# A fused attention and MLP kernel: five engine queues ordered by a list scheduler, softmax sums taken from a column of V, and merges, broadcasts and transposes moved to DMA

## Chip, cores, metric

One core of a Trainium2 chip. The metric is device time in microseconds (us) of one execution. The kernel before takes 318.04 us (median of 4 runs, 317.15 to 318.21).

Engines are named as in the profile: PE is TensorE (PEld its weight loads), DVE VectorE, ACT ScalarE, POOL GpSimd, SP the engine that issues most DMAs. Each engine has its own queue of instructions, and one that waits at the head of its queue holds up those behind it (below, DVE from 7.4 to 18.87 us in the control). A run counts as slow when it is over 1.5% above the fastest of the same kernel; comparisons use fast runs.

## The reference

x is normalised (layernorm, 2048 x 512) to xn; the output is x plus attention of xn plus an MLP of xn.

```python
# attention: 32 heads of 16, 4 segments of 512 positions, causal inside a segment
for s in range(N):
    logits = einsum('bhqd,bhkd->bhqk', qs, ks) * scale + mask
    a_dot = einsum('bhqk,bhkd->bhqd', softmax(logits), vs)
    pq = phi(qs)                         # phi(t) = t+1 if t>0 else exp(t)
    num = einsum('bhld,bhde->bhle', pq, M)
    den = einsum('bhld,bhd->bhl', pq, z)[..., None] + 1e-06
    outs.append(g * num / den + (1.0 - g) * a_dot)      # g = sigmoid(beta)
    M = M + einsum('bhld,bhle->bhde', phi(ks), vs)
    z = z + einsum('bhld->bhd', phi(ks))
o = concat(outs) @ wo
# MLP: silu(xn @ w1) @ w2, w1 is 512 x 1792
return x + o + mlp
```

## The kernel before

Scores are kept transposed (keys on partitions). Four heads are scored at once into `psS`, which fills four banks of PSUM (TensorE's output memory; the program divides it into eight), and one exp of 128x2048 empties it; there are 80 such quads, five for each of 16 groups (4 segments x 4 head groups). Both kernels have this loop and only one `psS`, so score, exp, next score form a serial chain.

```python
def s_quad(st, dt, quad, tiles):
    psS = psatt.tile([P, 4, L], F32, name="psS")
    ...  # 4 or 8 row-tiled matmuls
    Pt = ppool.tile([P, 4, L], BF16, name="Pt")
    nc.scalar.activation(out=Pt[:], in_=psS[:], func=AF.Exp, scale=SCALE)
    ...  # POOL masks the diagonal blocks a little later
```

The softmax sums are a second pass of one-hot matmuls over the same probabilities; the reciprocals are taken on 128x512 and replicated over the 16 rows of a head by matmuls with `sel`:

```python
def z_part(st, dt, tiles):          # as long as the product with V itself
    for par in (1, 0):
        for kt in KTS:
            for g in range(4):
                nc.tensor.matmul(psZ[32*g:32*g+32, kt*P:L], lhsT=oneh[:, 2*dt+par, :],
                                 rhs=p_view(tiles, par, g, kt), ...)
    ...
    nc.vector.reciprocal(out=rec[:], in_=zf[:])

def norm_fill(s, st):               # for each head group dt
    nc.tensor.matmul(psD, lhsT=sel[:, 1, dt, :], rhs=rec[:])   # 1/den, replicated
    pq = phiQT * psD
    nc.tensor.matmul(psR, lhsT=sel[:, 0, dt, :], rhs=rec[:])   # 1/sum, replicated
    a_t = N_sb * psR
    # later: psN = Mbf.T @ pq on PE, oT = a_t + psN on DVE
```

(`norm_fill` is shortened here.) PE's order is made by a cooperative loop: after each quad, generators are pulled until a virtual clock of PE time has passed 2.43 us; small work of other engines is delayed by `later(ns, fn)`.

The softmax here doesn't subtract the row's maximum and nothing guards it: scores larger than these inputs give would overflow.

Of the kernel before, what the change touches and what calls it, by code (L numbers as in the profile page):

```python
# [10 lines left out]
ALU = mybir.AluOpType  # L11
# [17 lines left out]
EPS = 1e-5  # L29

HRING = 23
FILL_NS = 2000
WARM = 44
# [3 lines left out]
def kernel(  # L37
# [17 lines left out]
    cpool = ctx.enter_context(tc.tile_pool(name="cpool", bufs=1))  # L55
    segp = ctx.enter_context(tc.tile_pool(name="segp", bufs=2))
    ppool = ctx.enter_context(tc.tile_pool(name="ppool", bufs=8))
    hpool = ctx.enter_context(tc.tile_pool(name="hpool", bufs=HRING))
    work = ctx.enter_context(tc.tile_pool(name="work", bufs=2))
    xpool = ctx.enter_context(tc.tile_pool(name="xpool", bufs=3))  # L60
    pp = ctx.enter_context(tc.tile_pool(name="pp", bufs=3, space=bass.MemoryType.PSUM))
    psz = ctx.enter_context(tc.tile_pool(name="psz", bufs=1, space=bass.MemoryType.PSUM))
    psatt = ctx.enter_context(tc.tile_pool(name="psatt", bufs=1, space=bass.MemoryType.PSUM))
    ctx.enter_context(tc.manual_schedule(engines={ENG.PE}))


    xts = {}

    def load_x(s, half):
        xt = xpool.tile([P, 2, D], BF16, name="x_in")  # L70
        r0 = s * L + half * 256
        nc.sync.dma_start(
            out=xt[:], in_=x_flat[r0 : r0 + 256, :].rearrange("(two p) d -> p two d", p=P)
        )
        xts[(s, 2 * half)] = xt[:, 0, :]
        xts[(s, 2 * half + 1)] = xt[:, 1, :]

    wk_sb = cpool.tile([P, DT, D], BF16, name="wk_sb")
    wq_sb = cpool.tile([P, DT, D], BF16, name="wq_sb")
    wv_sb = cpool.tile([P, DT, D], BF16, name="wv_sb")  # L80
    wo_sb = cpool.tile([P, DT, D], BF16, name="wo_sb")
    w1_sb = cpool.tile([P, DT, F], BF16, name="w1_sb")
    w2_sb = cpool.tile([P, FT, D], BF16, name="w2_sb")
    load_x(0, 0)
    load_x(0, 1)
    for dst, src in ((wk_sb, A_wk), (wq_sb, A_wq), (wv_sb, A_wv)):
        nc.sync.dma_start(out=dst[:], in_=src.rearrange("(ko ki) n -> ki ko n", ki=P))
    load_x(1, 0)
    for dst, src in ((w1_sb, B_w1), (wo_sb, A_wo), (w2_sb, B_w2)):
        nc.sync.dma_start(out=dst[:], in_=src.rearrange("(ko ki) n -> ki ko n", ki=P))  # L90
    load_x(1, 1)


    ident = cpool.tile([P, P], BF16, name="ident")
    make_identity(nc, ident[:])
    lnc = cpool.tile([P, 2, 2], F32, name="lnc")
    nc.gpsimd.memset(lnc[:, :, 0:1], EPS)
    nc.gpsimd.memset(lnc[:, :, 1:2], -0.5)

    pm_odd = cpool.tile([P, 1], F32, name="pm_odd")  # L100
    nc.gpsimd.memset(pm_odd[:], 1.0)
    for g in range(4):
        nc.gpsimd.memset(pm_odd[32 * g : 32 * g + 16, :], 0.0)




    clock = {"vt": 0.0, "n": 0}
    held = []

    def run_due():
        while held and held[0][0] <= clock["vt"]:
            heapq.heappop(held)[2]()

    def pe(ns):
        clock["vt"] += ns
        run_due()

    def later(ns, fn):
        clock["n"] += 1  # L120
        heapq.heappush(held, (clock["vt"] + ns, clock["n"], fn))


    xnT = {}
    mv_all = cpool.tile([P, NT, nc.vector.BN_AGGR_DIM], F32, name="mv_all")
    rstd_all = cpool.tile([P, NT, 1], F32, name="rstd_all")

    def ln_stats(s, half):
        t0 = s * TPS + 2 * half
        for j in range(2):  # L130
            stats = work.tile([P, nc.vector.BN_STATS_DIM], F32, name="stats")
            nc.vector.bn_stats(out=stats[:], in_=xts[(s, 2 * half + j)])  # L132
            nc.vector.bn_aggr(out=mv_all[:, t0 + j, :], in_=stats[:])
        rs = rstd_all[:, t0 : t0 + 2, :]
        nc.gpsimd.tensor_tensor(
            out=rs, in0=mv_all[:, t0 : t0 + 2, 1:2], in1=lnc[:, :, 0:1], op=ALU.add
        )
        nc.gpsimd.tensor_tensor(out=rs, in0=rs, in1=lnc[:, :, 1:2], op=ALU.pow)

    def ln_norm(s, j):  # L140
        t = s * TPS + j
        xn_t = work.tile([P, D], BF16, name="xn_t")
        nc.vector.tensor_scalar(  # L143
            out=xn_t[:], in0=xts[(s, j)],
            scalar1=mv_all[:, t, 0:1], scalar2=rstd_all[:, t, 0:1],
            op0=ALU.subtract, op1=ALU.mult,
        )
        return xn_t

    def ln_tr(s, j, xn_t, on_act=False):  # L150
        if s not in xnT:
            xnT[s] = segp.tile([P, DT, L], BF16, name="xnT")
        ptr = pp.tile([P, 4, P], BF16, name="ptr", tag="ps")
        for dt in range(DT):
            nc.tensor.transpose(ptr[:, dt, :], xn_t[:, dt * P : (dt + 1) * P], ident[:])  # L155
        pe(300)
        dst = xnT[s][:, :, j * P : (j + 1) * P]
        if on_act:
            nc.scalar.copy(out=dst, in_=ptr[:, :, :])
        else:  # L160
            nc.vector.tensor_copy(out=dst, in_=ptr[:, :, :])

    ln_done = set()

    def ln_fill(s):
        ln_stats(s, 0)
        ln_stats(s, 1)
        prev = None
        for j in range(TPS + 1):
            yield  # L170
            if prev is not None:
                ln_tr(s, j - 1, prev)
            prev = ln_norm(s, j) if j < TPS else None
        ln_done.add(s)


    def gemm4(lhsTs, rhss):
        ps = pp.tile([P, L], F32, name="ps", tag="ps")
        for ki in range(DT):
            nc.tensor.matmul(  # L180
                ps[:, :], lhsT=lhsTs(ki), rhs=rhss(ki), start=(ki == 0), stop=(ki == DT - 1)
            )
        pe(860)
        return ps

    def phi_part(src, dst, after, acc=None):
        ek = work.tile([P, L], BF16, name="ek")
        nc.scalar.activation(out=ek[:], in_=src, func=AF.Exp)  # L188

        def mn():  # L190
            nc.gpsimd.tensor_scalar(  # L191
                out=ek[:], in0=ek[:], scalar1=1.0, scalar2=0.0, op0=ALU.min, op1=ALU.max
            )
            later(800, fin)

        def fin():
            nc.vector.scalar_tensor_tensor(  # L197
                out=dst, in0=src, scalar=0.0, in1=ek[:], op0=ALU.max, op1=ALU.add, accum_out=acc
            )
            if after is not None:  # L200
                later(1000, after)

        later(900, mn)

    vts = []
    for i in range(2):
        vts.append(cpool.tile([P, TPS, H // 2, 3, DH], BF16, name=f"V{i}"))

    def start_proj(s, st):
        st["kT"] = segp.tile([P, DT, L], BF16, name="kT")  # L210
        st["kTo"] = segp.tile([P, DT, L], BF16, name="kTo")
        st["qT"] = segp.tile([P, DT, L], BF16, name="qT")
        st["V"] = vts[s % 2]
        if s < NSEG - 1:
            st["phiK"] = segp.tile([P, TPS, D], BF16, name="phiK", bufs=1)
            st["zc"] = segp.tile([P, DT], F32, name="zc")
        if s > 0:
            st["phiQT"] = segp.tile([P, DT, L], BF16, name="phiQT")

    def k_tile(s, st, dt):  # L220
        ps = gemm4(lambda ki: wk_sb[:, ki, dt * P : (dt + 1) * P], lambda ki: xnT[s][:, ki, :])
        kT, kTo = st["kT"], st["kTo"]
        if s == 0:
            nc.scalar.copy(out=kT[:, dt, :], in_=ps[:, :])
            nc.vector.tensor_scalar(  # L225
                out=kTo[:, dt, :], in0=ps[:, :], scalar1=pm_odd[:, 0:1], scalar2=None, op0=ALU.mult
            )
        else:
            nc.vector.tensor_copy(out=kT[:, dt, :], in_=ps[:, :])
            later(  # L230
                800,
                lambda: nc.gpsimd.tensor_scalar(
                    out=kTo[:, dt, :], in0=kT[:, dt, :], scalar1=pm_odd[:, 0:1], scalar2=1.0,
                    op0=ALU.mult, op1=ALU.mult,
                ),
            )
        if s < NSEG - 1:
            phiKT = work.tile([P, L], BF16, name="phiKT")

            def k_transposes():  # L240
                ptr = pp.tile([P, 4, P], BF16, name="ptr", tag="ps")
                for j in range(TPS):
                    nc.tensor.transpose(ptr[:, j, :], phiKT[:, j * P : (j + 1) * P], ident[:])
# [25 lines left out]
    def proj_fill(s, st, dt0=0):  # L269
        if dt0 == 0:  # L270
            start_proj(s, st)
# [492 lines left out]
```

## Time and profile before

| | before |
|---|---|
| start of the first exp | 21.8 us |
| start of the last exp | 276.4 us, so 254.6 / 79 = 3.22 us per exp |
| end of the last exp to the end of the span | 37.7 us |
| PE, ACT, DVE, POOL busy | 84, 63, 57, 43% |

First the page: busy time of each engine, the clock granted to PE in 40 slices (in tenths of full speed; 9 is 90% or more), the chain of work that ended last, and the exp group (count, then busy us and mean ns of one, then the idle time before it and what ended it).

```profile
span 316.0 us, 6029 instructions
## 1 busy us (share of the span) xinstructions
PE 265.2 (84%) x2496; PEld 117.2 (37%) x2496; DVE 179.7 (57%) x306; ACT 198.0 (63%) x172; POOL 137.0 (43%) x254
...
PEclk9589999999999799999997999999999999997999
...
PE 56%; DVE 22%; POOL 9%; issue 5%; ACT 5%; DMA 1%; POOLq 0%; ACTq 0%
...
L466 ACT ACTIVATE Pt<-psS 128x2048 bf16<-128x2048 f32 x80 | 150.1, 1876 | 57.4 <-PE psS L458 54.0
```

PE is the busiest and has most of the chain, and ACT waited 54.0 us for scores. Next, the stretch from first to last exp and the tail, from the windows view (columns: length in us, then busy us and instructions of each engine, granted clock, share of the 16 DMA engines, GB/s):

```profile
core 0: us, PE busy (x) PEld busy (x) DVE busy (x) ACT busy (x) POOL busy (x), PEclk, DMA share, GB/s
21.80:276.40 254.60, 223.85 (x2235) 96.54 (x2234) 148.51 (x259) 188.79 (x161) 118.56 (x185) 0.99 0.05 17
278.30:316.00 37.70, 29.98 (x182) 13.01 (x179) 18.31 (x24) 3.67 (x6) 1.09 (x1) 0.95 0.11 35
```

And from the timeline the shortest repeat of the loop (start us, length us, engine, line, operation, and the idle time before it):

```profile
140.71 1.88 ACT L466 ACTIVATE Pt<-psS 128x2048 bf16<-128x2048 f32 x1 [1.15 <-PE psS L458]
...
142.70 0.40 PE L458 MATMUL psS<-qT,kT 16*128 16x512 bf16 x4
...
143.20 1.88 ACT L466 ACTIVATE Pt<-psS 128x2048 bf16<-128x2048 f32 x1 [0.62 <-PE psS L458]
```

Where PE is ready, exps start 2.5 us apart: 1.88 us of exp and a gap of 0.62 us in which the score is made. The average is 3.22 us. The other 0.7 us is put down mostly to PE being occupied with something else when the next score is due; PE's 56% of the chain fits that.

### The profile page before, as it was taken

To read this page: it belongs to the slowest core of one execution; us is meant where nothing else is said; L and a number is where in the kernel's file an instruction comes from. 1 tells how busy PE (TensorE), PEld (TensorE's weight loads), DVE (VectorE), ACT (ScalarE), POOL (GpSimd) and SP (SyncE) were. 2 spreads that over 40 slices of the span, in tenths; PEclk is the share of its full clock that TensorE was granted. 3 is DMA by queue.
4 is the path that set the end of the run, shared out by engine and by line. 5 is a ranking of instruction groups with operands and counts; after the bars stand their busy time and mean duration, and the time that the engine had idled before them with its cause. 6 is when DMAs were issued, how large, how long until landed. Compare 5 with 4: busy or idle time off the path is not lost.

```text
span 316.0 us, 6029 instructions
## 1 busy us (share of the span) xinstructions
PE 265.2 (84%) x2496; PEld 117.2 (37%) x2496; DVE 179.7 (57%) x306; ACT 198.0 (63%) x172; POOL 137.0 (43%) x254
## 2 busy tenths in 40 slices
PE   5277869999977887899987889899989799997993
PEld 4122434443433433344333334344423243442441
DVE  3469998877475659411476474751565523237642
ACT  1048658988977497566993856676766578833000
POOL 4995647967333479533231244843323223310000
PEclk9589999999999799999997999999999999997999
DMA  6990010000000000021100000002020011020003
GB/s 220 385 340 21 0 36 33 2 3 0 2 0 2 0 3 1 2 68 33 35 0 2 0 3 0 2 0 68 2 66 2 0 35 34 2 68 0 0 0 100
DMA packets 11403, 12.44 MB, mean 39 GB/s; under 512 B 881, under 2 KB 10865, under 8 KB 11377
## 3 DMA queue, kind: packets, MB, share of 16 engines
q1 hardware_dynamic: 11376, 12.07, 11.8%
q8 instruction: 19, 0.31, 0.4%
q14 instruction: 8, 0.06, 0.1%
HBM read 9.97 MB, written 2.10 MB: 38 GB/s over the span
## 4 chain that ended last, share of the span: by engine, by line
PE 56%; DVE 22%; POOL 9%; issue 5%; ACT 5%; DMA 1%; POOLq 0%; ACTq 0%
PE ps L180 15%; PE psO L401 12%; PE psS L458 6%; PE psZ L519 5%; PE psO_3943 L401 4%; PE psPV L500 4%; DVE hT L301 4%; PE psO L410 3%; ACT Pt L466 2%; ACT th L295 2%; POOL w_sb L570 2%; DVE rec L541 2%; DVE stats L132 2%; DVE phiKT L197 2%; DVE phiQT L197 2%
## 5 line engine op out<-in xcount | busy, mean ns | idle before, releaser
L466 ACT ACTIVATE Pt<-psS 128x2048 bf16<-128x2048 f32 x80 | 150.1, 1876 | 57.4 <-PE psS L458 54.0
L478 POOL TENSOR_SCALAR_AFFINE_SELECT Pt<-Pt 128x512 bf16<-128x512 bf16 (+1 forms) x112 | 77.9, 708 | 120.9 <-ACT Pt L466 120.8
L180 PE MATMUL ps<-xnT,w_sb 128*128 128x512 bf16 x224 | 57.9, 391 | 8.1 <-DVE hT L301 7.5
L301 DVE SCALAR_TENSOR_TENSOR hT<-th,ps 128x512 bf16<-128x512 bf16 x56 | 37.5, 680 | 34.8 <-ACT th L295 34.3
L401 PE MATMUL psO<-w_sb,hT 128*128 128x512 bf16 x168 | 41.9, 383 | 0.0
L295 ACT ACTIVATE th<-ps 128x512 bf16<-128x512 f32 x56 | 32.9, 598 | 7.8 <-DVE hT L301 4.7
L401 PEld LDWEIGHTS <-hT 128*128 128x128 bf16 x224 | 21.2, 99 | 31.2 <-issue 9.1
L180 PEld LDWEIGHTS <-w_sb 128*128 128x128 bf16 x224 | 19.6, 99 | 34.8 <-issue 18.7
L458 PE MATMUL psS<-qT,kTo 32*128 32x512 bf16 (+3 forms) x256 | 17.7, 308 | 4.3 <-ACT Pt L466 2.6
L416 DVE TENSOR_TENSOR o_t<-psO,x_res 128x512 bf16<-128x512 f32 x12 | 8.2, 685 | 21.9 <-PE psO L410 21.9
L519 PE MATMUL psZ<-Pt,oneh 128*32 128x128 bf16 (+3 forms) x512 | 20.3, 300 | 0.0
L180 PE MATMUL ps<-xnT,wq_sb 128*128 128x512 bf16 x64 | 16.7, 384 | 3.5 <-DVE qT L259 3.5
L180 PE MATMUL ps<-xnT,wk_sb 128*128 128x512 bf16 x64 | 17.3, 395 | 1.9 <-DVE kTo L225 1.2
L458 PE MATMUL psS<-qT,kT 16*128 16x512 bf16 (+3 forms) x256 | 17.1, 300 | 1.1 <-ACT Pt L466 1.1
L191 POOL TENSOR_SCALAR ek<-ek 128x512 bf16<-128x512 bf16 x24 | 15.5, 651 | 4.1 <-ACT ek L188 4.1
L180 PE MATMUL ps<-wv_sb,xnT 128*128 128x512 bf16 x64 | 16.0, 379 | 1.3 <-DVE N_sb L509 0.8
L155 PE MATMUL ptr<-ident,xn_t 128*128 128x128 bf16 x64 | 6.9, 248 | 11.3 <-DVE xn_t L143 10.2
L541 DVE RECIPROCAL rec<-zf 128x512 bf16<-128x512 f32 x4 | 13.4, 3351 | 4.5 <-ACT zf L536 4.5
L509 DVE CAST N_sb<-psPV 128x512 bf16<-128x512 f32 x16 | 11.0, 686 | 8.8 <-PE psPV L500 8.7
L132 DVE BATCH_NORM_STATS2 stats<-x_in 128x6 f32<-128x512 bf16 x16 | 10.4, 678 | 9.6 <-DMA x_in<-in_A_x_dram 9.3
L519 PEld LDWEIGHTS <-oneh 128*32 128x32 bf16 x512 | 11.5, 96 | 10.3 <-issue 5.0
L458 PEld LDWEIGHTS <-kTo 32*128 32x128 bf16 x256 | 5.4, 92 | 22.4 <-issue 20.2
(92 smaller groups left out, 324.9 us busy)
## 6 DMA issues: line engine op xcount, KB each, us to landing
w_sb<-in_B_w_dram SPq DMA_DIRECT2D x2, 1792.0 KB, 13.8
x_in<-in_A_x_dram SPq DMA_DIRECT2D x8, 256.0 KB, 4.0
x_res<-in_A_x_dram SPq DMA_DIRECT2D x16, 128.0 KB, 2.2
out_dram<-o_t SPq DMA_DIRECT2D x16, 128.0 KB, 1.7
wk_sb<-in_A_wk_dram SPq DMA_DIRECT2D x1, 512.0 KB, 6.0
wq_sb<-in_A_wq_dram SPq DMA_DIRECT2D x1, 512.0 KB, 7.0
wv_sb<-in_A_wv_dram SPq DMA_DIRECT2D x1, 512.0 KB, 7.9
wo_sb<-in_A_wo_dram SPq DMA_DIRECT2D x1, 512.0 KB, 12.1
```

Of the source, the lines that this page charges most:

```text
L132: nc.vector.bn_stats(out=stats[:], in_=xts[(s, 2 * half + j)])
L180: nc.tensor.matmul(ps[:, :], lhsT=lhsTs(ki), rhs=rhss(ki), start=(ki == 0), stop=(ki == DT - 1))
L191: nc.gpsimd.tensor_scalar(out=ek[:], in0=ek[:], scalar1=1.0, scalar2=0.0, op0=ALU.min, op1=ALU.max)
L197: nc.vector.scalar_tensor_tensor(out=dst, in0=src, scalar=0.0, in1=ek[:], op0=ALU.max, op1=ALU.add, accum_out=acc)
L295: nc.scalar.activation(out=th[:], in_=ps[:, :], func=AF.Tanh)
L301: nc.vector.scalar_tensor_tensor(out=hT[:], in0=th[:], scalar=1.0, in1=ps[:, :], op0=ALU.add, op1=ALU.mult)
L401: nc.tensor.matmul(psO, lhsT=st["hT"][ft][:, j * P : (j + 1) * P], rhs=w2_sb[:, ft, :], start=(ft == 0), stop=False,)
L458: nc.tensor.matmul(psS[:, g, c : c + nq], lhsT=kk[r0:r1, dt, kt * P : (kt + 1) * P], rhs=st["qT"][r0:r1, dt, kt * P : L], start=True, stop ...
L466: nc.scalar.activation(out=Pt[:], in_=psS[:], func=AF.Exp, scale=SCALE)
L478: nc.gpsimd.affine_select(out=v, in_=v, compare_op=ALU.is_ge, fill=0.0, base=0, pattern=[[0, v.shape[1]], [1, P]], channel_multiplier=-1,)
L519: nc.tensor.matmul(psZ[32 * g : 32 * g + 32, kt * P : L], lhsT=oneh[:, 2 * dt + par, :], rhs=p_view(tiles, par, g, kt), start=(dt == 0 and ...
L541: nc.vector.reciprocal(out=rec[:], in_=zf[:])
```

## The change

It is a rewrite, meant to take work off PE and to order all queues for a 2.5 us loop. Its core, with cuts marked:

```diff
+T0 = 12.5          # when the first quad is due, us
+CYC = 2.5          # us per quad
+class Sched:       # list scheduler, run while the kernel is built
+    def add(self, eng, dur, fn, deps=(), due=0.0, vis=None, ...):
+        ...  # dur: us the engine is held; vis: us until the result can be used
+    def run(self):
+        ...  # per engine, take the ready task with the least due time;
+        ...  # exps and scores first; ACT takes a small task only if it fits before the next exp
+    ctx.enter_context(tc.manual_schedule(
+        engines={ENG.PE, ENG.Activation, ENG.DVE, ENG.Pool, ENG.SP}))
...
-        for j in range(TPS):                  # PE transposes of phi(K), of xn
-            nc.tensor.transpose(ptr[:, j, :], phiKT[:, j*P:(j+1)*P], ident[:])
+        nc.sync.dma_start(out=phiK_b[s].tile[:, :, dt*P:(dt+1)*P], in_=pb.tile[:], transpose=True)
+        e = A("SP", 0.5, f_t, [f], Dn(5*u + 9), vis=3.0, ...)
...
-    def z_part(st, dt, tiles): ...            # 512 one-hot matmuls
+    V_t = [sb([P, TPS, (H // 2) * PW], BF16, f"V{i}") for i in range(2)]   # PW = 33:
+    # even head, a column of ones, odd head; a product with 32 of these columns gives 16 rows
+    # of values and a row of sums
...
+    def norm(s, dts, due, due_rep):           # sums to DRAM, back as 128x128
+        nc.sync.dma_start(out=dap(dZ[s], ...), in_=src[16 - par : P : 32, 0:nd, :])
+        nc.sync.dma_start(out=Zg[w][0:np_, :], in_=dap(dZ[s], 0, [[P, np_], [1, P]]))
+        ...  # 4 DMAs merge odd heads into the even heads' tile
+        nc.vector.reciprocal(out=Zf[w][0:np_, :], in_=Zg[w][0:np_, :])
+        ...  # times (1 - g) on POOL, to DRAM, and back replicated over 16 partitions:
+        nc.sync.dma_start(
+            out=rb.tile[:, 0:nd, :].rearrange("p a b -> p (a b)"),
+            in_=dap(dR[s], 0, [[nd * L, 8], [0, DH], [1, nd * L]]))
+        d4 = A("SP", 0.5, f_6, [d3], due + 1, vis=3.5, ...)
+        ...  # N *= R on DVE, psN on PE, N += psN on DVE
+    def den(s, due): ...                      # the same round trip for 1/den (dD, dE, Dr)
...
+        k = A(eng, 0.5, fn, due=due, vis=2.6 + 0.4 * n, label=f"x{t}")     # loads of x
```

Also: the w1 scaling on POOL is gone (0.5 moves into the activation and the last eviction), x stays in SBUF instead of being loaded again as residual, evictions of the product with V double in number (even and odd heads), and the last output rows are summed in `psS`.

## The prediction

> **What bounds the kernel now.** The span is 316.0 us. The page gives PE 84% busy, ACT 63%, DVE 57%, POOL 43%; the chain that ended last is 56% PE, 22% DVE. The kernel has three stages (timeline): a start to the first 128x2048 exp at 21.8 us; 80 exps, the last starting at 276.4 us, so 254.6/79 = 3.22 us per exp; a tail of 37.8 us after the last exp ends at 278.2. One four-bank score tile makes score, exp, score serial: with TensorE ready, exps come 2.5 us apart (1.88 us exp, 0.62 us gap, room for one 0.6 us tanh). The other 0.7 us per exp are TensorE's: ACT waited 54 us for scores.
>
> TensorE's issue cost from the timeline: 0.216 us for a full 128x512 matmul, 1.20 us for 32 column-tiled ones, 0.33 us for a score quad plus 0.1 us of mode change. By instruction counts the middle holds about 219 us of such work in 254.6 us.
>
> **What changes.** Removed from TensorE: 512 one-hot sum matmuls (16 x 1.20 = 19 us), the replication matmuls (28 x 0.216 = 6 us), all but 16 of 112 transposes (about 7 us), 12 denominator matmuls in part (2 us), so about 33 us. Removed elsewhere: four 3.35 us reciprocals (now 128x128, about 0.85 us each), the 6.7 us w1 scaling on POOL. Added: 24 DMA transposes, DRAM round trips for sums and merges (x_res took 2.2 us a hop, so some 10 to 15 us per chain, an estimate), 16 more evictions at 0.69 us on DVE, 12 products on POOL. The Trainium skill, "VectorE: DVE Perf Modes", section "The three transpose paths", gives 1309 ns for a 128x128 DMA transpose; no transfer here shows it. My estimate is about 3 us for 128x512, off the critical path when issued early.
>
> Moved: the order. In the changed program's order, the middle holds about 616 full matmuls (133 us), 31 half-PV groups at 0.55 (17), scores (19), memory and denominators (4) and mode changes (19): about 192 us, 2.43 us per exp. So the 2.5 us score-exp loop becomes the bound, with TensorE close behind. ACT's order still has some gaps with two small activations (0.5 us more each), so I expect 2.6 us per exp, not 2.5.
>
> **Sum.** First exp about 16.5 us (five loads split over two queues, less POOL setup; cold-clock matmuls at 0.43 us remain). 79 x 2.61 + 1.9 = 208. Tail: about 95 full matmuls after the last exp, 20.6 us, plus PV, small waits and 3 us for the last eviction and store: about 25 us. Span 249.5, device time 2 us more: 251 us. Range 240 to 265. Faster by over 2%: 0.95; within 2%: 0.03; slower: 0.02.
>
> **What would show it.** Start-to-start of the 80 exps near 2.6 us, ACT waiting on scores some 40 us or less in the middle, PE busy near 85 to 90%, DVE near 70%; the psZ, psR, psD and psM-per-tile groups gone; first exp near 16 us; tail near 25 us.
>
> **What would make it wrong.** A DMA transpose much slower than 3 us, or the in-order SP queue holding a needed transfer behind one that waits: TensorE would then stall at the projections, the memory product or the output rows. Static order in which a late tanh or kTo (1.04 us on POOL here) delays an exp every cycle: 2.75 us would add 11 us. More dips of the granted clock (0.97 now).

## The result and the profile after

The first four runs gave 297.08 us median (291.91 to 298.29), a ratio to before of 0.925 (95% interval 0.916 to 0.933): faster, but 46 us above the prediction and outside its range. Two of the runs were fast (291.91, 296.08). Ratios here are the mean time of one kernel's fast runs over that of the other's fast runs of the same rounds, so not quite the ratio of the medians quoted.

The profile taken with that result fell on a slow run (298.29 us). The same kernel, run again as the control of the experiments (k0 below), left the profile of a fast run (289.77 us), and that is the one read here. Its page, with the lines that answer to those of before:

```profile
span 288.1 us, 4744 instructions
## 1 busy us (share of the span) xinstructions
PE 240.2 (83%) x1882; PEld 95.5 (33%) x1882; DVE 162.2 (56%) x283; ACT 194.4 (67%) x168; POOL 137.7 (48%) x201
...
PEclk9656999999999999999889899999978699999998
...
PE 40%; DMA 26%; DVE 17%; SPq 5%; POOL 5%; ACT 4%; issue 2%; DVEq 0%; ACTq 0%
...
L712 ACT ACTIVATE Pt<-psS 128x2048 bf16<-128x2048 f32 x80 | 150.3, 1878 | 41.1 <-PE psS L463 39.7
```

Its windows, from first to last exp and the tail:

```profile
core 0: us, PE busy (x) PEld busy (x) DVE busy (x) ACT busy (x) POOL busy (x), PEclk, DMA share, GB/s
27.70:255.60 227.90, 205.05 (x1680) 77.68 (x1679) 140.07 (x242) 185.01 (x156) 125.48 (x154) 0.96 0.21 43
257.40:288.10 30.70, 21.80 (x109) 9.18 (x108) 11.14 (x16) 4.00 (x8) 1.09 (x1) 0.96 0.08 30
```

ACT still waited 39.7 us for scores, the chain now has 26% DMA in it (before, 1%), and the granted clock is below full in slices where it was full before. In the three parts:

| | before | predicted | after (k0) |
|---|---|---|---|
| start of the first exp, us | 21.8 | 16.5 | 27.7 |
| first to last exp, us | 254.6 | 206.2 (79 x 2.61) | 227.9 (79 x 2.88) |
| end of the last exp to the end, us | 37.7 | 25 | 30.7 |
| span, us | 316.0 | 249.5 | 288.1 |

The three misses, 11.2, 21.7 and 5.7 us, add up to the 38.6 us between the predicted span and this one.

The middle is the interesting part. Of the 79 distances between exp starts, 68 average 2.63 us, what was predicted for all. The other 11 are over 3.2 us, and what they hold above 2.6 us comes to 20.4 us together. So the loop works as intended, and then stops a few times. In the timeline these stops stand at, or right behind, a wait of 1.7 to 6.8 us for a transfer. For one of them (the distance that starts at 194.1 us) the view names PE, but POOL's first product with Dr started there at 194.03 us, 6.5 us after Dr was issued, about as long as that broadcast takes; so this wait too is taken to be one for Dr.

**The start.** DVE in the timeline:

```profile
6.70 0.70 DVE L532 TENSOR_SCALAR xn<-x_all,mv,rstd 128x512 bf16<-128x512 bf16 x2
18.87 0.70 DVE L514 BATCH_NORM_STATS2 st<-x_all 128x6 f32<-128x512 bf16 x1 [11.47 <-DMA x_all<-in_A_x_dram]
...
19.70 0.66 DVE L558 CAST xnT<-ps 128x512 bf16<-128x512 f32 x1
```

After two of the four normalised tiles of segment 0, DVE's next instruction is the first statistics of segment 1, whose load (the chain view: 4.06 us to 18.84 us) was issued behind the 1.8 MB of w1. The evictions of segment 0's transposes, ready long before, stand behind it and run at 19.70 us. The schedule had assumed 4.2 us for this load (2.6 + 0.4 x 4). It took 14.8.

**A double stop in the middle.** Timeline around the broadcasts Dr (1/den) and R (1/sum) of one segment:

```profile
152.24 1.15 POOL L895 TENSOR_TENSOR pq<-pq,Dr 128x512 bf16<-128x512 bf16 x1 [4.30 <-DMA Dr<-dE]
...
153.95 2.26 POOL L895 TENSOR_TENSOR pq<-pq,Dr 128x512 bf16<-128x512 bf16 x2
...
156.16 1.09 POOL L726 TENSOR_SCALAR_AFFINE_SELECT Pt<-Pt 128x1024 bf16<-128x1024 bf16 x1
...
157.31 0.51 PE L463 MATMUL ps<-Pt,V 128*32 128x384 bf16 x12 [2.87 <-POOL Pt L726]
...
158.20 1.88 ACT L712 ACTIVATE Pt<-psS 128x2048 bf16<-128x2048 f32 x1 [3.50 <-PE psS L463]
...
159.54 2.73 DVE L957 TENSOR_TENSOR N<-N,R 128x512 bf16<-128x512 bf16 x4 [6.76 <-DMA R<-dR]
...
162.20 0.68 DVE L772 CAST O<-ps 128x512 bf16<-128x512 f32 x1
...
162.93 1.01 PE L463 MATMUL ps<-xnT,w_q 128*128 128x512 bf16 x2 [3.81 <-DVE O L772]
...
164.59 1.88 ACT L712 ACTIVATE Pt<-psS 128x2048 bf16<-128x2048 f32 x1 [4.03 <-PE psS L463]
```

Read it as two queues. POOL waited 4.30 us for Dr before its first product `pq`; three more products then sit around the mask that the next product with V needs, so the mask runs at 156.16 us, PE waits 2.87 us for it in the middle of that product, and ACT idles 3.50 us before the next exp. Meanwhile DVE waited 6.76 us for R; four products with R follow, and only then the eviction of O that frees a PSUM bank: PE waited 3.81 us for it, and ACT idled 4.03 us before the exp after that. PE itself needed neither R nor Dr at that moment. The broadcasts take about twice the scheduled 3.5 us; the chain view of another segment shows a hop by hop account (start us, length us):

```profile
86.81 2.03 DMA Zg<-dZ
...
90.33 1.44 DMA dR<-Zr
...
91.78 6.21 DMA R<-dR
```

In the double stop itself R was later still: the hop `dR<-Zr`, issued while the broadcast of Dr was under way, took 4.78 us there (the schedule had 2.2), and the broadcast 6.75 us.

While PE stands still its clock goes too. Windows of the idle stretch and of the one after it (same columns as above):

```profile
159.20:162.90 3.70, 0.00 (x0) 0.00 (x0) 3.36 (x6) 1.37 (x2) 2.46 (x3) 0.99 0.00 0
162.90:167.50 4.60, 4.57 (x20) 1.37 (x19) 3.54 (x6) 2.40 (x2) 0.96 (x1) 0.64 0.00 0
```

The 4.6 us after the 3.7 us without a matmul ran at 0.64 of full clock. The Trainium skill, "TensorE: Matmul & The Clock Gate", section "What's actually happening", says that the array falls to half rate after an idle window of about 3.4 us. This trace agrees with the direction and roughly the size.

**The tail.** TensorE's last output rows in banks 2 and 3 of `psS`, with the waits in brackets:

```profile
264.10 1.24 PE L463 MATMUL psS<-w,hT 128*128 128x512 bf16 x5 [1.36 <-DVE Rf L1093]
267.19 1.89 PE L463 MATMUL psS<-w,hT 128*128 128x512 bf16 x8 [1.85 <-DVE Rf L1093]
269.65 0.59 PE L463 MATMUL psS<-w,hT 128*128 128x512 bf16 x2 [0.58 <-DVE a L1097]
270.82 1.24 PE L463 MATMUL psS<-w,hT 128*128 128x512 bf16 x5 [0.57 <-DVE a L1097]
```

Four waits, 4.4 us, on VectorE reading banks 0 and 1 of the same tile.

### The profile page after: what moved, and what is told of

It reads as the page before. It is cut to its first block, busy times and chain, and to the rows that moved or that the text cites. A ratio compares the mean times of both kernels' runs of the same rounds, so it can differ in the third digit from the quotient of the medians.

```text
span 296.6 us, 4710 instructions
## 1 busy us (share of the span) xinstructions
PE 240.9 (81%) x1848; PEld 96.3 (32%) x1882; DVE 163.1 (55%) x283; ACT 194.4 (66%) x168; POOL 136.8 (46%) x201
## 4 chain that ended last, share of the span: by engine, by line
PE 37%; DMA 30%; DVE 16%; POOL 5%; ACT 4%; issue 3%; SPq 3%; DVEq 0%; ACTq 0%; POOLq 0%
PE ps L463 30%; DMA R<-dR 9%; PE psS L463 7%; DMA x_all<-in_A_x_dram 6%; DMA Dr<-dE 5%; DMA dR<-Zr 3%; ACT Pt L712 3%; DVE N L957 3%; SPq L925 2%; DMA Zg<-dZ 2%; POOL Pt L726 2%; POOL pq L895 2%; DMA dD<-den 2%; DMA xnT<-xn 2%; DMA Dg<-dD 2%
## 5 line engine op out<-in xcount | busy, mean ns | idle before, releaser
L726 POOL TENSOR_SCALAR_AFFINE_SELECT Pt<-Pt 128x1024 bf16<-128x1024 bf16 (+1 forms) x80 | 74.8, 935 | 86.7 <-ACT Pt L712 86.7
L463 PE MATMUL ps<-xnT,w 128*128 128x512 bf16 x211 | 58.5, 394 | 2.2 <-DVE hT L991 0.9
L463 PE MATMUL ps<-w,hT 128*128 128x512 bf16 x189 | 49.5, 393 | 3.2 <-DVE O L772 2.6
L991 DVE SCALAR_TENSOR_TENSOR hT<-hT,ps 128x512 bf16<-128x512 bf16 x56 | 37.5, 678 | 24.3 <-ACT hT L987 24.1
L987 ACT ACTIVATE hT<-ps 128x512 bf16<-128x512 f32 x56 | 32.8, 595 | 6.6 <-PE ps L463 6.6
L463 PE MATMUL ps<-Pt,V 128*32 128x128 bf16 (+3 forms) x512 | 25.6, 309 | 8.9 <-POOL Pt L726 7.7
L463 PEld LDWEIGHTS <-w 128*128 128x128 bf16 x224 | 20.4, 100 | 27.2 <-issue 9.3
L463 PE MATMUL ps<-xnT,w_k 128*128 128x512 bf16 x60 | 19.6, 413 | 4.1 <-DMA xnT<-xn 2.3
L463 PE MATMUL ps<-xnT,w_q 128*128 128x512 bf16 x62 | 19.2, 409 | 3.9 <-DVE O L772 3.5
L895 POOL TENSOR_TENSOR pq<-pq,Dr 128x512 bf16<-128x512 bf16 x12 | 13.8, 1155 | 12.3 <-DMA Dr<-dE 12.3
L463 PE MATMUL ps<-w_v,xnT 128*128 128x512 bf16 x61 | 18.4, 406 | 0.2 <-issue 0.2
L463 PE MATMUL psS<-qT,kTo 32*128 32x256 bf16 (+3 forms) x256 | 18.1, 315 | 0.2
L772 DVE CAST N<-ps 128x512 bf16<-128x512 f32 x15 | 10.3, 685 | 13.6 <-PE ps L463 13.4
```

What stands on the lines that cost most here:

```text
L463: nc.tensor.matmul(o, lhsT=l, rhs=r, start=start, stop=stop, **k)
L726: nc.gpsimd.affine_select(out=v, in_=v, compare_op=ALU.is_ge, fill=0.0, base=0, pattern=pat, channel_multiplier=-1,)
L772: nc.vector.tensor_copy(out=dst.tile[:, dt, :], in_=buf.tile[:])
L895: nc.gpsimd.tensor_tensor(out=pb.tile[:], in0=pb.tile[:], in1=rb.tile[:, dt, :], op=ALU.mult)
L987: nc.scalar.activation(out=hb.tile[:], in_=b.tile[:], func=AF.Tanh, scale=0.5)
L991: nc.vector.scalar_tensor_tensor(out=hb.tile[:], in0=hb.tile[:], scalar=1.0, in1=b.tile[:], op0=ALU.add, op1=ALU.mult)
```

## Experiments

Each kernel ran 4 times (k9: 6), with the kernel before on the same chip; k0 to k3 ran on one chip, k4 to k7 on a second, k8 to k10 on a third. "Excess" is the sum, over distances between exp starts above 3.2 us, of what exceeds 2.6 us; it and the first exp are read from each kernel's timeline, the clock from its profiled run. All results were correct. Medians are of all runs, ratios of fast runs alone; differences in us between two kernels are, in the text below, the difference of their ratios times 318 us, since the control had two slow runs of four.

| run | edit | median us | ratio to before (95%) | first exp us | excess us | clock |
|---|---|---|---|---|---|---|
| k0 | none (control) | 294.42 | 0.913 (0.904-0.922) | 27.7 | 20.4 | 0.937 |
| k1 | figure: x loads 15 us | 286.66 | 0.898 (0.894-0.902) | 19.2 | 27.1 | 0.949 |
| k2 | figure: broadcasts 7.3 us | 284.02 | 0.889 (0.883-0.895) | 27.8 | 12.6 | 0.920 |
| k3 | broadcast reads 16 rows | 279.07 | 0.873 (0.868-0.879) | 26.9 | 11.5 | 0.963 |
| k4 | tail sums in own banks | 287.76 | 0.905 (0.899-0.911) | 26.5 | 24.3 | 0.940 |
| k5 | k1 + k3 + k4 | 277.94 | 0.865 (0.858-0.873) | 18.1 | 22.7 | 0.963 |
| k6 | k5, figure: broadcasts 4.7 us | 267.00 | 0.839 (0.834-0.843) | 19.4 | 9.2 | 0.964 |
| k7 | k6, figures: transposes, beta | 258.92 | 0.814 (0.810-0.818) | 18.7 | 4.1 | 0.987 |
| k8 | all figures, nothing else | 264.43 | 0.830 (0.825-0.834) | 16.4 | 8.1 | 0.987 |
| k9 | k7, figure: w1 13.5 us | 263.22 | 0.824 (0.820-0.827) | 16.1 | 7.7 | 0.981 |
| k10 | k7, figure: broadcasts 7.3 us | 262.01 | 0.821 (0.816-0.827) | 16.8 | 5.8 | 0.993 |

The profiled runs of k5 and k9 were slow runs; their medians and ratios stand, but their last three columns are only indications. The theory is that figures in the schedule which were too low put consumers of late transfers in front of urgent work. The rivals are that the transfers are simply too slow for the buffers there are, whatever the order, and for the tail and the start, causes on PE or in the load traffic.

### k0, the control

> The changed kernel again, as the control for the other runs of this call. All theories expect what its first runs gave: 292 to 298 us, first exp near 26.9 us, broadcasts from DRAM near 6.9 us each, and a mean granted clock near 0.92 to 0.94.

Measured: 289.8 to 295.3 us, two runs of four slow. It held, except that one run was 2.2 us below the expected range and the first exp 0.8 us later.

### k1, true landing time for the later x loads

```diff
-        k = A(eng, 0.5, fn, due=due, vis=2.6 + 0.4 * n, label=f"x{t}")
+        k = A(eng, 0.5, fn, due=due, vis=(2.6 + 0.4 * n) if n == 1 else 15.0, label=f"x{t}")
```

> Only the scheduler's figure for the landing of the later x loads changes (15 us instead of 4.2; the profile showed 14.1). Theory: the 10 us hole at the start comes from the static DVE order, which puts the next segment's first statistics, waiting for a load that lands at 18.1 us, ahead of this segment's evictions; so the first exp moves from 26.9 to about 16 to 18 us and the time falls by 8 to 11 us. Rival: the loads themselves are late for the first segment or the weights are; then the first exp stays above 24 us and the time moves by less than 3 us.

Measured: 4.8 us below the control; first exp at 19.2 us instead of 27.7. The loads are the same, only the order changed, so the hole was one of order. Of the 8.5 us won at the start, part was lost again in the middle (excess 27.1 instead of 20.4 us), so the gain is under the expected 8 to 11 us. The first exp is later than expected: the beta load, which the schedule had landing after 3 us, took 8.5 us, and POOL (the multiply with beta) and DVE waited for it in the same manner.

### k2, true landing time for the broadcasts

```diff
-        d4 = A("SP", 0.5, f_6, [d3], due + 7, vis=3.5, ...)      # Dr
+        d4 = A("SP", 0.5, f_6, [d3], due + 7, vis=7.3, ...)
-        d4 = A("SP", 0.5, f_6, [d3], due + 1, vis=3.5, ...)      # R
+        d4 = A("SP", 0.5, f_6, [d3], due + 1, vis=7.3, ...)
```

> Only the scheduler's figure for the two 512 KB broadcasts from DRAM changes (7.3 us instead of 3.5; the profile showed 6.9). The transfers stay as they are. Theory 1, static order: the five gaps of 4 to 7.5 us between exps come from work put in front of masks and evictions on POOL and DVE as if the broadcast had landed; with the true figure the order moves it, the gaps shrink to under 4 us, and the time falls by 12 to 25 us. Theory 2, latency: the chain itself is too long for the buffers, so the gaps move elsewhere and the time falls by less than 6 us.

Measured: 7.7 us below the control; excess from 20.4 to 12.6 us. That lies between the two theories' ranges (12 to 25, under 6 us). It did not bring the gaps under 4 us as expected: three of 8.3, 4.9 and 4.9 us remained. The longest has another cause, a transposed tile that took 7.3 us (the chain view), with 3.0 in the schedule; it was issued at 139.89 us, 2.0 us after a broadcast of Dr:

```profile
139.89 7.32 DMA xnT<-xn
```

### k3, the broadcast from 16 rows

```diff
-            nc.sync.dma_start(out=dap(dR[s], 0, [[P, np_], [1, P]]), in_=Zr[w][0:np_, :])
+            for c in range(2):
+                nc.sync.dma_start(
+                    out=dap(dR[s], c * nd * L, [[2 * nd * L, 8], [P, np_ // 8], [1, P]]),
+                    in_=Zr[w][0:np_, :])
...
-                in_=dap(dR[s], 0, [[nd * L, 8], [0, DH], [1, nd * L]]),
+                in_=dap(dR[s], 0, [[nd * L, 16], [0, DH // 2], [1, nd * L]]),
```

and the same for dE and Dr; the schedule's figures for the doubled store rise with it (SP 0.5 to 1.0 us, landing 2.2 to 2.7). The Trainium skill, "DMA: Bandwidth & Descriptors", section "Rules for kernel authors", says that an outermost size under 16 confines a DMA to at most that many of the 16 engines.

> The replicated reciprocals are stored twice in DRAM so that each broadcast reads 16 rows 8 times instead of 8 rows 16 times; same bytes, one more 32 KB store each. The schedule's figures stay (3.5 us for the broadcast). Theory: the outermost count of 8 keeps the transfer on half of the DMA engines (their mean busy share was 0.35 to 0.42 while one ran); with 16 it lands in about 4 to 4.5 us and the time falls by 10 to 20 us. Rival: the transfer is bound by something else, stays near 6.9 us, and the time stays within 3 us of the control.

Measured: 12.6 us below the control. A broadcast of R in the chain view, with the hop before it:

```profile
203.96 1.92 DMA dR<-Zr
...
205.95 4.40 DMA R<-dR
```

It took 4.40 us against 6.2 to 7.0 for 512 KB in the control. Windows inside one broadcast of R, the control's first, then k3's (the last two columns are the share of the DMA engines and GB/s):

```profile
213.00:218.50 5.50, 4.89 (x41) 1.72 (x39) 0.69 (x1) 5.49 (x5) 1.73 (x2) 0.91 0.42 98
```

```profile
206.00:210.00 4.00, 3.47 (x37) 1.30 (x36) 1.38 (x2) 3.98 (x5) 1.73 (x2) 1.00 0.50 135
```

98 GB/s became 135. In another broadcast of k3 the share was 0.61 over 247 to 250 us, where a store of 128 KB also ran, and still 0.64 over the last of these us, which 8 engines of 16 cannot give. So the trace agrees with the page, though it does not list the engines used. The same bytes, landing 2 to 3 us sooner, took 12.6 us off the kernel. (The store's new figures may have shifted the order too; that share is not separated.)

### k4, the tail's sums in their own banks

```diff
-                mm(psS[:, 0, :], sel[:, k, :], EO[:, k, :], k == 0, k == 1)
+                mm(zb.tile[:], sel[:, k, :], EO[:, k, :], k == 0, k == 1)
...
-                nc.vector.reciprocal(out=Rf[:, c], in_=psS[:, 0, c])
+                nc.vector.reciprocal(out=Rf[:, c], in_=zb.tile[:, c])
```

> The changed kernel with one part edited: the tail's replicated sums and values of the last head group go to two banks of their own instead of banks 0 and 1 of the score tile, into whose banks 2 and 3 the last output rows are summed. Theory: in the tail TensorE waited 1.3, 1.9, 0.6 and 0.6 us for VectorE to finish reading the score tile, though in other banks, because the waits are kept by tile; without it the stretch from the end of the last exp to the end falls from 30 us by 3 to 5 us. Rival: the tail is bound by the matmuls and their cold clock; then it falls by less than 1.5 us.

Measured: 287.76 us; from the end of the last exp (259.8 us) to the end (285.1) it is 25.3 us instead of 30.7. In the timeline the four waits are gone:

```profile
262.72 1.03 PE L463 MATMUL ps<-EO,sel 128*128 128x512 bf16 x4
263.59 1.03 PE L463 MATMUL psS<-w,hT 128*128 128x512 bf16 x4
...
265.31 2.75 PE L463 MATMUL psS<-w,hT 128*128 128x512 bf16 x12
```

The tail was 5.4 us shorter, while the middle had 3.9 us more excess in the profiled run; the whole was 2.5 us faster, and the two intervals overlap, so only the tail's part is shown. The edit also let the sums go ahead of the last exp, but they did not: they start 3.0 us after its end in the control and 2.9 us here. So VectorE's reads of one bank had held up TensorE's writes to others, because both belonged to one tile.

### k5, three edits together

> Three edits together: true figure for the later x loads (k1), 16 source rows in the broadcast (k3), the tail in its own banks (k4); the schedule still has 3.5 us for the broadcast, which took 3.9 to 4.5 us in k3. If the parts add up, 294 - 8 - 15 - 4 = 267 us; if they share the same slack, above 272 us.

Measured: 277.94 us (fast runs 273.9 and 277.1), far from the 267 expected of a plain sum and in the other range, above 272; by ratios too, the three gains add up to 0.850 and 0.865 was measured. The start gain is there. In the tail the control's four waits are gone, but it is 30.0 us long, with 121 matmuls in it instead of 109. The middle is as bad as the control's. The edits change the order, and the broadcasts, 4.3 to 6.0 us here where they met other transfers, still land after the schedule's 3.5; POOL waited 7.6 us for one of them.

### k6, and the true figure for the faster broadcast

> As k5, and the schedule now has 4.7 us for the broadcast. Static-order theory: fewer gaps over 3.2 us between exps than in k5 and 2 to 6 us less time (262 to 266 us). Rival, the latency of the chain is what counts: within 1.5 us of k5.

Measured: 8.5 us less than k5, with the same transfers; excess 9.2 us instead of 22.7. The direction is the theory's and the size above the 2 to 6 us expected.

### k7, and true figures for transposes and beta

```diff
-                e = A("SP", 0.5, f_d, [n], due, vis=3.0, ...)      # DMA transposes (2 places)
+                e = A("SP", 1.25, f_d, [n], due, vis=3.5, ...)
-        "SP", 0, 3.0,                                              # load of beta
+        "SP", 0, 9.0,
```

> As k6, and the schedule now has 1.25 us of SP time and 3.5 us to landing for each DMA transpose (it had 0.5 and 3.0; SP was held 1.2 us by each) and 9 us for the beta load (it had 3; 8.5 were seen in k1). Theory: first exp near 16.5 us instead of 19.2, and the waits of TensorE for a transposed tile (5.7 us in k2, 7.9 us in k1) go, so 3 to 8 us less than k6. Rival: they were noise of a crowded queue, and the time stays within 2 us of k6.

Measured: 258.92 us, 7.7 us less than k6, at the upper end of the expected gain. Its page:

```profile
span 258.9 us, 4718 instructions
...
PE 230.7 (89%) x1848; PEld 95.7 (37%) x1882; DVE 163.8 (63%) x283; ACT 195.0 (75%) x168; POOL 135.7 (52%) x201
...
PEclk9879999999999999999999999999999999999999
```

Four gaps above 3.2 us are left, and the clock is near full throughout. The first exp was not at 16.5 but at 18.7 us: PE's order had a projection with w1 before the first score, and w1 had been given 10 us but took 13.0 (the chain view: 3.84 us to 16.86). In the timeline:

```profile
16.91 1.20 PE L463 MATMUL ps<-xnT,w 128*128 128x512 bf16 x3 [2.03 <-DMA w<-in_B_w_dram]
```

### k8, only the figures

```diff
  the k1, k2 and k7 figures together; every DMA, buffer and operation as in the changed kernel
```

> Only numbers in the schedule change against the changed kernel, no transfer and no operation: later x loads 15 us, beta 9 us, DMA transposes 1.25 us of SP and 3.5 us to landing, broadcasts 7.3 us. Theory, wrong figures in a static order: most of the loss comes back, 264 to 272 us, granted clock above 0.96. Rival, the round trips themselves are too slow: 276 us or more (k1 and k2 together would give about 276).

Measured: 264.43 us, 26.6 us below the control. The profile shows a full clock in nearly all slices, and a broadcast that is still slow (the chain view):

```profile
span 262.5 us, 4743 instructions
...
PEclk9999999999999999999979999999997999999999
...
188.78 7.08 DMA R<-dR
```

Here the broadcasts still read 8 rows and still take about 7 us, and three waits in the tail (2.0 us of the control's 4.4) are still there. So the rival (too slow, whatever the order) is refuted for most of the loss. The longest distance left, 6.6 us at 195.1 us, stands at the broadcast shown: DVE waited 2.59 us for it; the hop before it had taken 4.09 us, where the schedule still had 2.2.

### k9, the figure for w1

> k7, and the schedule has 13.5 us for the landing of the w1 load (it had 10; 13.0 were seen in k7, where the first score stood behind a projection that waited for it). Theory: the first exp comes at 15.5 to 16.5 us instead of 18.7 and the time falls by 1 to 3 us. Rival: the cold clock of TensorE there hides it, within 0.7 us of k7 (258.9).

Measured: the first exp came at 16.1 us as expected, and the time rose by 3.0 us. Neither expectation held for the time. With the new figure the stops lie elsewhere, too: in the profiled run a distance of 5.7 us appeared, ending at 201 us. The broadcast of R in front of it landed as scheduled (4.69 us), and DVE waited only 1.08 us for it; but then its four products with R took 4.92 us (first line), where the same four took 1.43 us in the control at 98 us (second line):

```profile
194.25 4.92 DVE L964 TENSOR_TENSOR N<-N,R 128x512 bf16<-128x512 bf16 x4 [1.08 <-DMA R<-dR]
```

```profile
98.28 1.43 DVE L957 TENSOR_TENSOR N<-N,R 128x512 bf16<-128x512 bf16 x4 [1.97 <-DMA R<-dR]
```

POOL was busy for 4.7 of the 5.0 us from 194.2 us, and for 0.3 of the 1.4 us in the control. So a duration of DVE in the schedule (0.5 us for one product) can be wrong too; that POOL's work is the cause is not tested. A truer figure does not always give a better order; the scheduler takes each choice as it comes. The size of this lottery, judged by this run, is a few us.

### k10, a figure that is too high

> k7, and the schedule has 7.3 us for a broadcast that takes about 4.5. Theory: a figure that is too high costs little, since other work fills the time: within 2 us of k7. Rival: buffers are held longer in the schedule and the time rises by more than 3 us.

Measured: 2.3 us above k7; their profiled fast runs have spans of 259.2 and 258.9 us. It lies between the two expectations, and within the lottery of k9 it decides nothing, except that a figure 2.6 us higher than k7's cost far less than one 1.2 us lower had cost (k5 against k6, 8.5 us).

## Why the prediction was wrong

- **What bounded the kernel before**: right. With the sums, replications and transposes gone and the order in step with the transfers, the loop runs at 2.66 us per exp in k7 and 2.67 in k8; PE is busy for 191.9 us between first and last exp in k7 and 194.2 in k8 (windows view; k7's trace lacks some 30 of 1661 matmul records), against the 192 us counted. So the count of the work was right; what the program's order did with it was not foreseen.
- **The step that failed** is the sum of the middle: "79 x 2.61 + 1.9 = 208" has no term for a wait on a transfer. The prediction says "off the critical path when issued early" of the DMA transposes, and its sum treats the round trips of the sums in the same way. In their place the control shows 11 stops, 20.4 us of excess, out of 21.7 us missed in the middle. The chain of round trips was sized about right ("10 to 15 us"; from the issue of `dZ<-O` to the landing of R, 13.4 to 19.2 us in the control), and a risk was named: "the in-order SP queue holding a needed transfer". SP's part was small (the transposed tile at 138.5 us was issued 1.7 us after it was written, behind others that held SP 1.2 us each, and PE then waited 2.29 us for it). The long stops came from POOL and DVE, with consumers of the broadcast placed ahead of masks and evictions. The prediction nowhere weighs the landing times written into the change. The slowest hop, 512 KB replicated out of 8 rows with `vis=3.5`, has no counterpart in the trace before, but that trace did show 512 KB loads landing in 6.0 to 12.1 us (several at once), w1 and w2 in 13.8 (median; the change has 10 for w1) and beta in 6.8 (the change has 3).
- **"First exp about 16.5 us"**: measured 27.7. The loads were named and then only counted as help ("five loads split over two queues"). In the program's order, DVE's fifth statistics stand ahead of segment 0's evictions; this was visible before the run, beside 1.8 MB of w1 issued ahead of that load. k1 (19.2) and k8 (16.4 us), which change only figures, show that it was order.
- **"Tail ... about 25 us"**: measured 30.7. The term "small waits" was mis-sized: 4.4 us of waits for VectorE on another bank of the same tile. k4 gave 25.3. (The length of the tail also depends on how much work the order leaves for it: 28.1 us in k7, with 121 matmuls instead of 107.)
- **"More dips of the granted clock"** came true (0.937 against 0.967 before), but as a consequence of the order: k8, which changes only figures, has 0.987. Clock and excess do not go together run by run: k2 has less excess than the control and a clock of 0.920.
- **A slow DMA transpose**: not the main cause. It took about 2.5 us to land (the prediction had 3) and held SP 1.2 us. Its figures mattered when it met broadcasts (k2's 7.3 us; k6 to k7, where beta's figure changed too, so its own share stays open).
- **ACT waiting on scores "some 40 us or less"** was met (39.7 us) in spite of the miss, so it was a poor test: 0.6 us of each loop is such a wait anyway. The distribution of distances was the right one.

What stays open: how much of the excess in each kernel is wait and how much slow clock after it, what the slower DVE products cost (k9), and why the changed kernel varies by 2% from run to run where before varies by 0.3 to 1.1% on one chip. That its stops depend on DMA timing would fit, but k1, with the most excess, varies by 0.5%, and no run here tests it.

## What to carry to other kernels

A static order over in-order engines turns a wrong transfer time into a stop of engines that never needed the transfer, so check each assumed landing time against a trace before trusting the order. In the one case tried each way here, a figure that was too high cost 2.3 us (k10) and one that was too low 8.5 (k5 against k6). When a rewrite is judged in advance, the durations written into it are claims to be checked, above all those for transfers of a form that no trace shows yet. Judge such a loop by the distribution of its repeat times: the typical repeat was right from the start (2.63 us), and 11 of 79 carried the loss.

## What the Trainium skill lacked or had wrong

- "DMA: Bandwidth & Descriptors", "Anatomy of one DMA — SWDGE (gpsimd) path": its fit of 2.0 us plus bytes over 436 GB/s is for DMAs issued by the gpsimd engine and would give 3.2 us for 512 KB (an estimate from that fit). The broadcast from DRAM here, issued by SP, took 6.2 to 7.0 us from 8 rows and 4.4 us from 16. The rule on outermost sizes in the same page fits the direction but gives no time, and the fit does not mention it.
- "VectorE: DVE Perf Modes", "The three transpose paths": 1309 ns for 128x128. Here 128x512 landed in about 2.5 us alone (2.48 at 70.36 us in the control) and in 7.3 us beside a broadcast (k2), and held the issuing queue for 1.2 us; that section gives neither.
- "TensorE: Matmul & The Clock Gate", "What's actually happening": an idle window of about 3.4 us is named. In the kernel before, 2.0 us without a matmul (286.1 to 288.1 us) were followed by 3.1 us at 0.58 of full clock, so a shorter idle time was enough.
- No page that was read says that the program makes reads and writes of different banks of one tile wait for each other; here that was 4.4 us (the control's tail, gone in k4).
